# The last block of an expert's tokens: rows of its capacity, or all 128 of its list

## The chip, the core and the metric

The kernel runs on one core of a Trainium2 chip. The metric is the device time of one execution in microseconds (us); the time before is the median of three runs, 435.78 us (433.74 to 437.44). A profiled execution of the same kernel took 432.73 us.

## What is computed

The reference is a retention layer (8 sequences of 576 positions, 8 heads of 64) and behind it a layer of 8 experts in which each token goes to one expert at most. Cut to what matters here:

```python
x = attn_out.transpose(0, 2, 1, 3).reshape(4608, 512)      # the tokens
do_compute = (x @ w_skip) > 0                               # about half of them go on
e_idx = argmax(x[do_compute] @ w_gate, axis=1)              # one expert each
for e in range(8):
    mask = e_idx == e
    h = maximum(xc[mask] @ w1[e], 0)                        # 512 -> 1024
    y[mask] = gate_w[mask, None] * (h @ w2[e])              # 1024 -> 512
out[do_compute] = xc + y
```

All inputs and outputs are 32-bit floats.

## The kernel before, in words

The first part, to about 180 us, computes the retention in groups of 128 tokens (36 groups), writes every token's row of 512 numbers to `out` in HBM, and on the way works out each token's expert and its place in that expert's list. The second part, the expert stage, goes over the experts in order of size, expert 0 being the largest. Each has a fixed capacity, `CAPS = (368, 344, 332, 308, 304, 286, 278, 276)`, and its list is worked on in three blocks of up to 128 rows. `blocks(e)` (L379) gives each block its number of rows `n`: 128, 128 and what is left of the capacity, so the last block has 112, 88, 76, 52, 48, 30, 22 and 20 rows for experts 0 to 7. What is over a capacity is worked on in a loop at the end (L965), which had no round to do in the profiled run.

The list itself (`gidx`, from `slot_ids`, L336) always has 3 x 128 entries for each expert, since every token's place is compared with `iota`, which counts to 384. An entry that no token holds comes out as 0, which is the row of the first token (`max(id - 128, 0)`, L361).

For one expert the steps are:

- gather (L793, through `fetch`, L302): one indirect DMA for each block, on GpSimd's queue, reads the rows of the listed tokens from `out` into `xg[:n, k, :]`, a row on each partition. Expert 0's first two blocks are fetched earlier (L296, with a list of their own), and its last one in `slot_ids` (L351). An expert's gather is issued while the expert before it, or the one before that, is at work.
- turn (L797): TensorE transposes the block so that the 512 features lie on the partitions. The 512 features are four groups of 128 columns (`cs`); for each group and block one transpose takes `xg[:n, k, 128 columns]` as weights and a piece of the unit matrix, `ident[:n, :n]`, as the moving operand. The result lands in a PSUM bank `pt`. Then `split` (L143) writes it as two parts: ScalarE rounds it into `xhi`, VectorE subtracts that from it into `xlo`. One turn call of experts 1 to 7 does one column group, all three blocks; there are four such calls, put between the products of the expert before (L885, `turn_next`). Expert 0's last block is turned alone, in two calls of two column groups each (L938).
- up and down (L390, L809): products of `xhi`, `xlo` with the weights' parts `whi`, `wlo`, three for each pair, in 8 steps `f`. `up` goes into `ph`, is rounded through a relu into `hhi` and `hlo`, and `down` adds into `py`. Both take only the capacity's columns, `xT[:, c, :CAPS[e]]`.
- finish (L833): the result is copied to `yT`, transposed back into `yn` (L840), scaled and added to `xg[:n]` (L842), and scattered to `out` by an indirect DMA, `n` rows (L843).

TensorE's order is written out by hand (`manual_schedule`, L667); the order of the other engines is the scheduler's. Weights come in chunks of 512 KB on SyncE's queue, up to five steps ahead (`AHEAD`), and are split on ScalarE (L139) and VectorE (L140).

In the profile L804 is the transposes of a turn, L144 and L145 its split, L303 every gather, L387 all products of up and down.

Of the kernel before, what the change touches and what calls it, by code (L numbers as in the profile page):

```python
# [23 lines left out]
P = 128  # L24
# [32 lines left out]
def kernel(  # L57
# [9 lines left out]
    nc = tc.nc  # L67
# [25 lines left out]
    ident = const.tile([P, P], F32, tag="ident", name="ident")  # L93
# [49 lines left out]
    def split(hi, lo, x):  # L143
        nc.scalar.copy(hi, x)  # L144
        nc.vector.tensor_tensor(lo, x, hi.bitcast(F32), ALU.subtract)  # L145
# [132 lines left out]
    xg0 = ep.tile([P, NBLK, DM], F32, tag="xg0", name="xg0")  # L278
# [23 lines left out]
    def fetch(dst, idx, nrow=NTOK):  # L302
        nc.gpsimd.indirect_dma_start(  # L303
            out=dst,
            out_offset=None,
            in_=out[:nrow],
            in_offset=bass.IndirectOffsetOnAxis(ap=idx, axis=0),
            bounds_check=nrow - 1,
            oob_is_err=False,
        )  # L310
# [21 lines left out]
    gidx = const.tile([P, NBLK, NE], I32, tag="gidx", name="gidx")  # L332
# [3 lines left out]
    def slot_ids(ps):  # L336

        info = ps[:, 0 : NBLK * NE * NCMP].rearrange("s (b e k) -> s b e k", b=NBLK, k=NCMP)
        pb = [P, NBLK, NE, NE]

        k, n = blocks(0)[-1]
        rl = rt.tile([P, NE, NCMP], F32, tag="rl", name="rl", bufs=1)
        nc.vector.tensor_copy(rl, info[:, k])
        il = rt.tile([P, NE], F32, tag="il", name="il")
        nc.vector.scalar_tensor_tensor(il, rl[:, :, 0], float(P), rl[:, :, 1], ALU.mult, ALU.add)
        nc.vector.tensor_tensor(il, il, lead, ALU.mult)
        ids = rt.tile([P, 1], F32, tag="ids", name="ids")
        nc.vector.tensor_reduce(ids, il, axis=AX.X, op=ALU.add)
        gl = rt.tile([P, 1], I32, tag="gl", name="gl")
        nc.vector.tensor_scalar(gl, ids, float(-P), 0.0, ALU.add, ALU.max)  # L350
        fetch(xg0[:n, k, :], gl[:n])  # L351
        raw = rt.tile([P, NBLK, NE, NCMP], F32, tag="raw", name="raw", bufs=1)
        nc.vector.tensor_copy(raw, info)
        idf = rt.tile([P, NBLK, NE], F32, tag="idf", name="idf")
        nc.vector.scalar_tensor_tensor(idf, raw[:, :, :, 0], float(P), raw[:, :, :, 1], ALU.mult, ALU.add)
        pm = rt.tile(pb, F32, tag="pm", name="pm")
        nc.vector.tensor_tensor(
            pm, idf.unsqueeze(2).broadcast_to(pb), perm.unsqueeze(1).broadcast_to(pb), ALU.mult
        )
        nc.vector.tensor_reduce(idf, pm, axis=AX.X, op=ALU.add)  # L360
        nc.vector.tensor_scalar(gidx, idf, float(-P), 0.0, ALU.add, ALU.max)  # L361
        far = rt.tile([P, NBLK, NE], F32, tag="far", name="far")
        nc.vector.tensor_scalar(far, idf, float(P), FAR, ALU.is_lt, ALU.mult)
        nc.vector.scalar_tensor_tensor(sidx, idf, float(-P), far, ALU.add, ALU.add)
        gs = rt.tile([P, NBLK, NE], F32, tag="gs", name="gs")
        nc.vector.tensor_tensor(gs, raw[:, :, :, 2], raw[:, :, :, 3], ALU.add)
        nc.vector.tensor_tensor(gs, gs, raw[:, :, :, 4], ALU.add)
        pg = rt.tile(pb, F32, tag="pg", name="pg")
        nc.vector.tensor_tensor(
            pg, gs.unsqueeze(2).broadcast_to(pb), perm.unsqueeze(1).broadcast_to(pb), ALU.mult  # L370
        )
        nc.vector.tensor_reduce(gate, pg, axis=AX.X, op=ALU.add)
# [6 lines left out]
    def blocks(e):  # L379
        return [(k, min(P, CAPS[e] - k * P)) for k in range(NBLK)]  # L380
# [368 lines left out]
    def bank(tag, name, bufs=1):  # L749
        return (pm if tag == "m" else mpp).tile([P, 512], F32, tag=tag, name=name, bufs=bufs)  # L750
# [41 lines left out]

    def gather(e, xg, ks):  # L793
        for k, n in ks:
            fetch(xg[:n, k, :], gidx[:n, k, e : e + 1])

    def turn(e, xg, hi, lo, ks, cs, tag):  # L797

        c0, c1 = ks[0][0] * P, ks[-1][0] * P + ks[-1][1]
        w = c1 - c0  # L800
        pt = bank(tag, f"pt_{e}_{cs[0]}_{c0}")[:, : len(cs) * w].rearrange("p (c i) -> p c i", i=w)
        for i, c in enumerate(cs):
            for k, n in ks:
                nc.tensor.transpose(  # L804
                    pt[:, i, k * P - c0 : k * P - c0 + n], xg[:n, k, c * P : (c + 1) * P], ident[:n, :n]
                )
        split(hi[:, cs[0] : cs[-1] + 1, c0:c1], lo[:, cs[0] : cs[-1] + 1, c0:c1], pt)

    def down(e, f, ks, py, h, w):  # L809
        if e == 0:  # L810
# [44 lines left out]
    def gather_next(e, xg):  # L855

        xg[e] = mp.tile([P, NBLK, DM], F32, tag="xg", name=f"xg_{e}", bufs=3)
        gather(e, xg[e], blocks(e))

    def experts(acts):  # L860
# [24 lines left out]
        def turn_next(e):  # L885
            xT[e] = [mp.tile([P, NCC, CAP], F32R, tag=x, name=f"{x}_{e}") for x in ("xhi", "xlo")]
            for c in range(NCC):
                where = ((5, 0), (6, 0), (6, 1), (7, 0))[c] if e == 1 else (3 + c, 0)
                at(e - 1, *where, lambda c=c: turn(e, xg[e], *xT[e], blocks(e), [c], ("pt", "m")[c % 2]))
# [4 lines left out]
        for n in range(len(steps) + 1):  # L894
# [33 lines left out]
            if last and last[2] is late:  # L928
                for f in range(NCUT):
                    down(0, f, late, py[0], hs[0, f], wq[0, f])  # L930
                split_raw(len(raw))
            elif last:
                e, f, ks = last
                if e not in py:
                    py[e] = [bank(f"py{c}", f"py_{e}_{c}") for c in range(NBLK if e == 0 else NCC)]
                if n == NCUT:
                    down(e, f, ks[:1], py[e], hs[e, f], wq[e, f])
                    for cs, tag in (((0, 1), "pt"), ((2, 3), "py3")):  # L938
                        turn(0, xg0, xhi0, xlo0, late, cs, tag)
                    ks = ks[1:]  # L940
                down(e, f, ks, py[e], hs[e, f], wq[e, f])
                if f == NFC - 1:
                    y = evacuate(e, py[e])
                    if e + 1 < NE:
                        for k, where in zip(blocks(e), ((1, 1), (2, 0), (2, 1))):
                            at(e + 1, *where, finish, e, y, xg[e], [k])
                    else:
                        finish(e, y, xg[e], blocks(e), ("pt", "m", "ph"))
# [5 lines left out]
    def rest():  # L954
        routing(0)
        slot_ids(ps_m)
        expert_ids()
        regs[1:] = expert_regs()[1:]
# [6 lines left out]
    with tc.For_i(0, nblock, 1):  # L965
# [28 lines left out]
        for c in range(NCC):  # L994
            turn(0, xg0, xhi0, xlo0, one, [c], ("pt", "py3")[c % 2])
# [69 lines left out]
```

## Time and profile before

| | |
|---|---|
| median of three runs | 435.78 us |
| profiled execution | 432.73 us, of it span 431.0 us |
| PE busy (matmuls) | 391.7 us, 91% of the span |
| transposes of the turns, L804 | 88: 56 of 128x128, 4 each of 112, 88, 76, 52, 48, 30, 22, 20 rows |
| gathers, L303 | 24 indirect DMAs, 948 to 2015 ns of GpSimd each |
| mean granted TensorE clock | 0.983 |

In the rows below, times are us from the span's start unless marked ns. PE is TensorE's matmuls, PEld its weight loads, which overlap the matmuls; DVE is VectorE, ACT ScalarE, POOL GpSimd. A matmul's start is recorded and its end is modelled, and matmuls overlap; so what an operation takes of PE's stream is read from one start to the next, and not from its length. A row "pt<-ident,xg 52*128 52x128" is an operation that writes or feeds `pt` from `ident` and `xg`, with 52 active rows and 128 columns of the array. "idle before <-" names what ended an engine's idle time; "issue" is time in which the profile shows nothing that it waited for.

### The profile page before, as it was taken

The page shows a single profiled execution, that of the slowest core. Times are in us where ns is not written, and L with a number is a line of the kernel's source. Part 1 is how long each engine was busy: PE and PEld are TensorE (multiplying, and loading weights), DVE is VectorE, ACT ScalarE, POOL GpSimd, SP SyncE. Part 2 cuts the span into 40 slices and gives each one's busy share as a digit, 9 for nine tenths or more (in the row PEclk, how much of TensorE's full clock was granted, in tenths as well). Part 3 has the DMA queues.
Part 4 walks back from the last instruction along what each step waited for, and adds up shares of the span by engine and source line. Part 5 has one row for each costly group of instructions (what it writes and reads, how often), then busy time and mean ns, then how long its engine had stood idle before and what let it go on. Part 6 is the DMA issues. An engine that isn't in the chain of part 4 may idle for free. (4 is left out here: it accounts for less than half of the span.)

```text
span 431.0 us, 13306 instructions
## 1 busy us (share of the span) xinstructions
PE 391.7 (91%) x5482; PEld 351.7 (82%) x5484; DVE 276.3 (64%) x562; ACT 186.9 (43%) x360; POOL 160.4 (37%) x182
## 2 busy tenths in 40 slices
PE   7788988899988589999999999999999999999990
PEld 3576776677777467888999999999999999999980
DVE  2595598488589978848755554865654755656430
ACT  2255444454644457117444434444444445445210
POOL 4665564545555397150330042033141250400302
PEclk9899999999999989999999999999999999999996
DMA  8899989899986977255673455455465465642101
GB/s 311 301 326 314 344 304 314 313 327 307 365 310 232 338 284 240 98 149 207 203 230 117 146 172 193 147 173 185 150 212 172 162 207 173 200 144 77 52 0 52
DMA packets 29023, 92.14 MB, mean 214 GB/s; under 512 B 4119, under 2 KB 4247, under 8 KB 28960
## 3 DMA queue, kind: packets, MB, share of 16 engines
q1 hardware_dynamic: 19584, 71.31, 48.4%
q0 software_dynamic: 3616, 9.86, 6.7%
q10 hardware_dynamic: 5760, 10.09, 6.3%
q8 instruction: 44, 0.72, 0.7%
q14 instruction: 19, 0.16, 0.1%
HBM read 77.07 MB, written 14.55 MB: 213 GB/s over the span
## 5 line engine op out<-in xcount | busy, mean ns | idle before, releaser
L140 DVE TENSOR_TENSOR wlo_w<-w,whi_w 128x1024 fp32r<-128x1024 f32 x59 | 71.9, 1223 | 61.9 <-ACT whi_w L139 61.8
L513 POOL TENSOR_TENSOR kn<-u,tt_sb 64x512 f32<-64x512 f32 x72 | 77.3, 1073 | 67.2 <-PE psc L479 44.2
L843 POOL DMA_INDIRECT out<-rs,sidx x24 | 32.8, 1366 | 156.4 <-DVE rs L842 153.2
L139 ACT CAST whi_w<-w 128x1024 fp32r<-128x1024 f32 x59 | 61.6, 1051 | 61.5 <-PE py L387 59.4
L542 ACT COPY u<-ps_s 64x256 f32<-64x256 f32 x128 | 47.0, 367 | 65.6 <-issue 26.7
L387 PE MATMUL py<-hhi,whi_w 128*128 128x344 f32 (+6 forms) x224 | 70.6, 315 | 0.0
L387 PE MATMUL ph<-xhi,whi_w 128*128 128x344 f32 (+6 forms) x224 | 68.9, 308 | 0.0
L387 PE MATMUL py<-hhi,wlo_w 128*128 128x344 f32 (+6 forms) x224 | 67.8, 303 | 0.0
L387 PE MATMUL ph<-xhi,wlo_w 128*128 128x344 f32 (+6 forms) x224 | 67.8, 302 | 0.0
L387 PE MATMUL ph<-xlo,whi_w 128*128 128x344 f32 (+6 forms) x224 | 67.7, 302 | 0.0
L387 PE MATMUL py<-hlo,whi_w 128*128 128x344 f32 (+6 forms) x224 | 67.6, 302 | 0.0
L531 PE MATMUL ps_s<-u,kn 64*64 64x64 f32 x1024 | 48.8, 227 | 14.4 <-issue 6.4
L531 PEld LDWEIGHTS ps_s<-u,kn 64*64 64x64 f32 x1024 | 39.2, 135 | 26.8 <-issue 10.8
L495 DVE TENSOR_TENSOR u<-psc,dt_sb 64x512 f32<-64x512 f32 x72 | 49.6, 689 | 14.2 <-PE psc L479 8.9
L395 ACT ACTIVATE hhi<-ph 128x344 fp32r<-128x344 f32 (+8 forms) x61 | 26.0, 427 | 64.1 <-PE ph L387 57.0
L479 PE MATMUL psc<-u 64*64 64x64 f32 x1152 | 51.8, 227 | 1.9 <-DVE u L495 0.6
L560 PE MATMUL pxt<-u 128*64 128x64 f32 x1152 | 45.1, 231 | 3.2 <-issue 2.8
L479 PEld LDWEIGHTS psc<-u 64*64 64x64 f32 x1152 | 41.7, 136 | 5.3 <-issue 2.4
L560 PEld LDWEIGHTS pxt<-u 128*64 128x64 f32 x1152 | 39.1, 142 | 7.5 <-issue 4.6
L387 PEld LDWEIGHTS py<-hhi,whi_w 128*128 128x128 f32 x224 | 42.2, 188 | 0.9
L387 PEld LDWEIGHTS ph<-xhi,whi_w 128*128 128x128 f32 x224 | 42.3, 189 | 0.1
L387 PEld LDWEIGHTS ph<-xlo,whi_w 128*128 128x128 f32 x224 | 42.3, 189 | 0.1
(178 smaller groups left out, 645.0 us busy)
## 6 DMA issues: line engine op xcount, KB each, us to landing
u<-qkv SPq DMA_DIRECT2D x72, 512.0 KB, 5.2
w<-w SPq DMA_DIRECT2D x64, 512.0 KB, 3.7
out<-xn ACTq DMA_DIRECT2D x36, 256.0 KB, 5.4
out<-rs,sidx POOLq DMA_INDIRECT x24
xg<-out,gidx POOLq DMA_INDIRECT x21
dt_sb<-dtab ACTq DMA_DIRECT2D x1, 256.0 KB
gt_sb<-dtab ACTq DMA_DIRECT2D x1, 256.0 KB
wg_sb<-wg ACTq DMA_DIRECT2D x1, 64.0 KB, 8.8
```

The source lines that it names most:

```text
L139: nc.scalar.copy(hi, t)
L140: nc.vector.tensor_tensor(lo, t, hi.bitcast(F32), ALU.subtract)
L387: nc.tensor.matmul(ps, x, y, start=first and n == 0, stop=last and n == 3 * len(terms) - 1)
L395: nc.scalar.activation(hi, ph, AF.Relu)
L479: nc.tensor.matmul(psc_t[g][halves[j], c, a, :], u[halves[j], 1 - j, c, a, :], u[halves[j], j, c, a, :], start=c == 0 and a == 0, stop=c = ...
L495: nc.vector.tensor_tensor(u_t[g][h, j], psc[halves[j]], dt_sb[h, c0 : c0 + 2], ALU.mult)
L513: nc.gpsimd.tensor_tensor(kn_t[g][h], u_t[g][h, 2 + j], tt_sb[h, 0, c0 : c0 + 2, :].unsqueeze(3).broadcast_to([D, 2, NPR, D]), ALU.mult,)
L531: nc.tensor.matmul(ps_s[halves[j], a, :], kn_t[g][h, c, a, :], u_t[g][h, 3 - j, c, a, :], start=n % NQ == 0 and a == 0, stop=a == NPR - 1, ...
L542: nc.scalar.copy(u_t[g][halves[j], 3 - j, c], ps_s[halves[j]])
L560: nc.tensor.matmul(pxt[halves[j], a, c * D : (c + 1) * D], u_t[g][:, 3 - j, c, a, :], u_t[g][:, j, c, a, :], start=c == 0 and a == 0, stop ...
L843: put = nc.gpsimd.indirect_dma_start(out=out, out_offset=bass.IndirectOffsetOnAxis(ap=sidx[:n, k, e : e + 1], axis=0), in_=rs[:n], in_offs ...
```

## The change

The gather of every block fetches 128 rows, whatever the capacity leaves for the block: the last block's gather takes all 128 entries of its list, in `gather` and, for expert 0, in `slot_ids`. Every transpose of a turn takes 128 rows and the whole unit matrix. The PSUM piece `pt` is as wide as the blocks times 128, and the split reads from it only the columns up to the capacity, as before. Nothing else reads the added rows: up, down and finish keep their sizes.

```diff
--- before.py
+++ after.py
@@ -348,7 +348,7 @@
         nc.vector.tensor_reduce(ids, il, axis=AX.X, op=ALU.add)
         gl = rt.tile([P, 1], I32, tag="gl", name="gl")
         nc.vector.tensor_scalar(gl, ids, float(-P), 0.0, ALU.add, ALU.max)
-        fetch(xg0[:n, k, :], gl[:n])
+        fetch(xg0[:, k, :], gl)
         raw = rt.tile([P, NBLK, NE, NCMP], F32, tag="raw", name="raw", bufs=1)
         nc.vector.tensor_copy(raw, info)
         idf = rt.tile([P, NBLK, NE], F32, tag="idf", name="idf")
@@ -792,19 +792,17 @@
 
     def gather(e, xg, ks):
         for k, n in ks:
-            fetch(xg[:n, k, :], gidx[:n, k, e : e + 1])
+            fetch(xg[:, k, :], gidx[:, k, e : e + 1])
 
     def turn(e, xg, hi, lo, ks, cs, tag):
 
         c0, c1 = ks[0][0] * P, ks[-1][0] * P + ks[-1][1]
-        w = c1 - c0
+        w = len(ks) * P
         pt = bank(tag, f"pt_{e}_{cs[0]}_{c0}")[:, : len(cs) * w].rearrange("p (c i) -> p c i", i=w)
         for i, c in enumerate(cs):
-            for k, n in ks:
-                nc.tensor.transpose(
-                    pt[:, i, k * P - c0 : k * P - c0 + n], xg[:n, k, c * P : (c + 1) * P], ident[:n, :n]
-                )
-        split(hi[:, cs[0] : cs[-1] + 1, c0:c1], lo[:, cs[0] : cs[-1] + 1, c0:c1], pt)
+            for k, _ in ks:
+                nc.tensor.transpose(pt[:, i, k * P - c0 : (k + 1) * P - c0], xg[:, k, c * P : (c + 1) * P], ident)
+        split(hi[:, cs[0] : cs[-1] + 1, c0:c1], lo[:, cs[0] : cs[-1] + 1, c0:c1], pt[:, :, : c1 - c0])
 
     def down(e, f, ks, py, h, w):
         if e == 0:
```

TensorE's order at expert 0's last block (`pt_0_256` and `pt_2_256` are its two PSUM pieces, `xg_130` is expert 0's tile; the shape is that of the output):

```order
 L387 MATMUL py_0_3337<-wlo_w_4_2989_3126,hhi_4_3502 128x512
 L387 MATMUL py_0_3337<-whi_w_4_2989_3125,hlo_4_3503 128x512
-L804 MATMUL pt_0_256_3528<-ident,xg_130 128x112 x2
-L804 MATMUL pt_2_256_3533<-ident,xg_130 128x112 x2
+L804 MATMUL pt_0_256_3528<-ident,xg_130 128x128 x2
+L804 MATMUL pt_2_256_3533<-ident,xg_130 128x128 x2
 L387 MATMUL py_1_3338<-whi_w_4_2989_3125,hhi_4_3502 128x512
 L387 MATMUL py_1_3338<-wlo_w_4_2989_3126,hhi_4_3502 128x512
```

The four transposes stand where they stood, and are of 128 columns in place of 112.

TensorE's order at the first column group of expert 3 (`xg_4094` its tile), which is turned among the products of expert 2:

```order
 L387 MATMUL ph_3_0_4233<-xlo_3894,whi_w_3_3995_3997 128x332
 L387 MATMUL ph_3_0_4233<-xhi_3893,wlo_w_3_3995_3998 128x332
-L804 MATMUL pt_0_0_4250<-ident,xg_4094 128x128 x2
-L804 MATMUL pt_0_0_4250<-ident,xg_4094 128x52
+L804 MATMUL pt_0_0_4250<-ident,xg_4094 128x128 x3
 L387 MATMUL py_0_4144<-hhi_2_4176,whi_w_2_3954_3956 128x332
 L387 MATMUL py_0_4144<-hlo_2_4177,whi_w_2_3954_3956 128x332
```

Three transposes as before, in the same place; the third has 128 columns in place of 52. The same holds for all column groups of experts 1 to 7.

GpSimd's order from expert 0's last gather on, before (`xg_3474`, `xg_3762`, `xg_4094` are the tiles of experts 1, 2 and 3; L843 is the scatter of expert 0's results):

```order
L303 DMA xg_130<-out,gl 112x512
L303 DMA xg_3474<-out,gidx 128x512 x2
L303 DMA xg_3474<-out,gidx 88x512
L303 DMA xg_3762<-out,gidx 128x512 x2
L303 DMA xg_3762<-out,gidx 76x512
L843 DMA out<-rs_0_3820,sidx 4608x512
L843 DMA out<-rs_1_3848,sidx 4608x512
L843 DMA out<-rs_2_3865,sidx 4608x512
L303 DMA xg_4094<-out,gidx 128x512 x2
L303 DMA xg_4094<-out,gidx 52x512
```

And in the changed kernel (L841 is the same scatter):

```order
L303 DMA xg_130<-out,gl 128x512
L303 DMA xg_3474<-out,gidx 128x512 x3
L303 DMA xg_3762<-out,gidx 128x512 x3
L841 DMA out<-rs_0_3820,sidx 4608x512
L841 DMA out<-rs_1_3848,sidx 4608x512
L841 DMA out<-rs_2_3865,sidx 4608x512
L303 DMA xg_4094<-out,gidx 128x512 x3
L841 DMA out<-rs_0_4165,sidx 4608x512
```

The number and the order of the DMAs are the same, and so are the waits of every engine; each last gather has 128 rows. Rows of one shape are now written as one.

## The prediction

> **What bounds the kernel now.** I read the page's head first, then busy time by stretch, then the waits, then the timeline around the turns. The head gives the span and the load of each engine.
>
> ```profile
> span 431.0 us, 13306 instructions
> PE 391.7 (91%) x5482; PEld 351.7 (82%) x5484; DVE 276.3 (64%) x562; ACT 186.9 (43%) x360; POOL 160.4 (37%) x182
> ```
>
> The windows view splits the expert stage, in which experts 1 to 7 are turned. Columns: stretch, its length, busy time and instructions of PE, PEld, DVE, ACT and POOL, granted clock, DMA share, GB/s.
>
> ```profile
> 214.00:243.00 29.00, 29.00 (x191) 28.93 (x190) 15.11 (x21) 13.58 (x21) 4.09 (x4) 1.00 0.54 178
> 304.00:334.00 30.00, 30.00 (x216) 29.12 (x215) 17.20 (x26) 13.99 (x22) 8.31 (x6) 1.00 0.51 175
> 364.00:393.00 29.00, 29.00 (x223) 28.14 (x222) 17.60 (x28) 14.15 (x23) 4.38 (x3) 1.00 0.52 166
> ```
>
> PE is busy for the whole of each stretch at a granted clock of 1.00; VectorE and ScalarE work about half of it and the DMA engines half. But a busy PE need not be a full PE, and the waits from 214 to 393 us say so (waiter, releaser, us in total, times, longest).
>
> ```profile
> ACT whi_w L139 <- PE py L387: 54.2, 42, 1.7
> DVE wlo_w L140 <- ACT whi_w L139: 58.4, 35, 2.0
> PEld pt L804 <- issue: 3.3, 20, 0.2
> ```
>
> The first two rows are engines that wait on PE, or behind one that does; none of the answer's rows has PE waiting for one of them. The third is PE's weight load standing idle 20 times at line 804, the turn, with nothing that the profile shows to wait for. Twenty is four column groups times five experts, and experts 3 to 7 are the five whose last block has fewer than 64 rows (52, 48, 30, 22, 20). The forms at that line are these.
>
> ```profile
> L804 PEld LDWEIGHTS pt<-ident,xg x88: 132/140/144, 185.3 to 385.4; 128*128 128x128 f32 x56, 112*128 112x128 f32 x4, 88*128 88x128 f32 x4, 76*128 76x128 f32 x4
> ```
>
> The timeline shows what a turn takes of PE's stream. Three turns follow: one for expert 2 (last block 76 rows), one for expert 3 (52), one for expert 7 (20). Its merged row "x3" is three blocks, the last the short one. Columns: start, length, engine, line, operation.
>
> ```profile
> 219.53 0.45 PE L804 MATMUL pt<-ident,xg 128*128 128x128 f32 x3
> 219.78 0.40 PE L387 MATMUL py<-hhi,whi_w 128*128 128x344 f32 x1
> 220.02 0.32 PE L387 MATMUL py<-hlo,whi_w 128*128 128x344 f32 x1
> 220.17 0.32 PE L387 MATMUL py<-hhi,wlo_w 128*128 128x344 f32 x1
> ...
> 252.00 0.57 PE L804 MATMUL pt<-ident,xg 128*128 128x128 f32 x3
> 252.50 0.42 PE L387 MATMUL py<-hhi,whi_w 128*128 128x332 f32 x1
> 252.76 0.32 PE L387 MATMUL py<-hlo,whi_w 128*128 128x332 f32 x1
> 252.91 0.32 PE L387 MATMUL py<-hhi,wlo_w 128*128 128x332 f32 x1
> ...
> 385.05 0.54 PE L804 MATMUL pt<-ident,xg 128*128 128x128 f32 x3
> 385.53 0.40 PE L387 MATMUL py<-hhi,whi_w 128*128 128x278 f32 x1
> 385.76 0.29 PE L387 MATMUL py<-hlo,whi_w 128*128 128x278 f32 x1
> 385.89 0.29 PE L387 MATMUL py<-hhi,wlo_w 128*128 128x278 f32 x1
> ```
>
> I charge a turn with the time from its first start to the second product behind it, less one usual spacing of products, because the first product behind a turn starts early and is held. With 76 rows: 220.02 - 219.53 - 0.15 = 0.34 us. With 52 rows: 252.76 - 252.00 - 0.15 = 0.61. With 20 rows: 385.76 - 385.05 - 0.13 = 0.58. Fewer rows cost more: a step between 76 and 52 rows. The weight loads show one half of it, a pause ahead of the short block.
>
> ```profile
> 252.31 0.13 PEld L804 LDWEIGHTS pt<-ident,xg 52*128 52x128 f32 x1 [0.17 <-issue]
> ...
> 374.36 0.13 PEld L804 LDWEIGHTS pt<-ident,xg 20*128 20x128 f32 x1 [0.17 <-issue]
> ```
>
> **The change part by part.** No instruction is added, dropped or moved, and no wait changes. Three things grow: the last block's transposes, its gathers, and the tile in PSUM that the split reads (still only the capacity's columns).
>
> *Transposes of experts 3 to 7.* What a full third block costs is not in the turns of before, but the same kind of transpose stands in the result's turning back, four of 128x128 in a row.
>
> ```profile
> 245.22 0.60 PE L840 MATMUL yn<-ident,yT 128*128 128x128 f32 x4
> 245.57 0.40 PE L387 MATMUL ph<-xhi,whi_w 128*128 128x332 f32 x1
> 245.81 0.32 PE L387 MATMUL ph<-xlo,whi_w 128*128 128x332 f32 x1
> 245.96 0.32 PE L387 MATMUL ph<-xhi,wlo_w 128*128 128x332 f32 x1
> ```
>
> By the same measure four cost 245.81 - 245.22 - 0.15 = 0.44 us, so one 0.11 and three 0.33. A turn of expert 3 so gains 0.61 - 0.33 = 0.28 us and one of expert 7 gains 0.58 - 0.33 = 0.25. With the mean of the ends, 0.265, twenty turns gain 5.3 us. All of it lies on PE, which ends last throughout this stretch, so it comes off the end one for one. What is late next: each step of a product pair is shortened by under 0.3 us four times per expert, while VectorE is busy 17.20 of 30 us and DMA 0.51 of it; neither comes near.
>
> *Transposes of experts 1 and 2.* 88 and 76 rows become 128: 0.34 before against 0.33 for three full ones, so nothing, and I bound the eight turns by one column's price. One full transpose spends 0.11 us on 128 columns, 0.86 ns each; 40 and 52 columns more, four times each, are at most 0.3 us. I take zero, from the row with 76.
>
> *Expert 0's turn and its late gather.* Here PE does wait for data. The gather is issued behind the list at 181.59 us and PE starts on it at 185.31, 3.7 us later.
>
> ```profile
> 181.59 1.29 POOL L303 DMA_INDIRECT xg<-out,gl  x1 [11.32 <-DVE gs L367]
> 185.31 0.57 PE L804 MATMUL pt<-ident,xg 112*128 112x112 f32 x4 [0.62 <-DMA xg<-out,gl]
> ...
> 185.83 1.06 POOL L303 DMA_INDIRECT xg<-out,gidx  x1 [0.31 <-issue]
> 193.14 0.46 PE L804 MATMUL pt<-ident,xg 128*128 128x128 f32 x3
> ...
> 354.70 0.95 POOL L303 DMA_INDIRECT xg<-out,gidx  x1 [0.30 <-issue]
> ...
> DMA packets 29023, 92.14 MB, mean 214 GB/s; under 512 B 4119, under 2 KB 4247, under 8 KB 28960
> ```
>
> Sixteen more rows of 2 KB are 32 KB; at the mean of 214 GB/s that is 0.15 us, and nothing if they ride beside the others. Four transposes grow by 16 columns of 0.86 ns, 0.05 us together. I take 0.1 us for both, range 0 to 0.2.
>
> *The other gathers.* POOL spends 1.06 us on the 88 rows issued at 185.83 and 0.95 us on the 20 rows at 354.70, so its time hardly hangs on the rows, and POOL is busy at most 28% of a stretch (8.31 of 30 us). What a gather lands later is covered: expert 1's last block, at 3.7 us from issue, is there at 189.5 and first used at 193.1; expert 7's at 358.4 and used at 374.36. Nothing on the path, as long as 3.6 us of cover hold. All capacities together gain 576 rows (16+40+52+76+80+98+106+108), 1.2 MB against 92.14.
>
> *Sum.* -5.3 + 0.1 = -5.2 us, with ends at -4.8 (full 0.3 at experts 1 and 2, and 0.2 at expert 0) and -5.3. The profiled execution took 432.73 us, its span and 1.73 us around it, so 427.5 by its own measure. It ran 0.7% below the median of the three timed runs, 435.78; on that scale the forecast is 430.6 us.
>
> A rule that speaks against the change stands in the Trainium skill, page "TensorE: Matmul & The Clock Gate", section "Why this matters for your kernels": a single matmul with a contraction of 32 takes as long as one with 128. By it the short blocks would hold nothing to win. The rows disagree: 0.61 us with 52 rows, 0.34 with 76.
>
> **The rivals.**
>
> *A, half the pause stays.* The 3.3 us ahead of the short block go, but the rest stays, because it belongs to the passage from transposes to products and not to the row count. Then 435.78 - 3.3 + 0.1 = 432.6 us. Against it: the passage behind four full transposes is in the 0.44 us already, and that is 0.11 each with nothing left over.
>
> *B, the gain is taken back.* With PE faster, the weights' way (load, round on ScalarE, subtract on VectorE) sets the pace: 435.8 us. Against it: ScalarE waits 54.2 us for PE in this stretch.
>
> *C, the length decides.* If a transpose costs by its columns and the pauses come of something that stays, 576 rows times four groups at 0.86 ns add 2.0 us: 437.8 us. For it: the four full transposes of line 840 do run at one even spacing of 0.11 us, so columns have a price. Against it: the five experts that pause are just the five under 64 rows. The Trainium skill's rule above points this way.
>
> *D, slower: the longer gathers land late.* The added list entries are mostly empty slots, which the kernel points to row 0, so many reads go to one row. If they were served one after another at r ns each, expert 1 (40 rows, cover 3.6 us) and expert 7 (108 rows, cover 374.36 - 358.4 = 16.0 us) would be the first to stop PE, from 90 and 148 ns on. At 200 ns that is 4.4 + 5.6 = 10.0 us, less the 5.2: 440.6 us, and experts 5 and 6 could only add. It turns the change to a loss from about 167 ns a row on. One of the 16 DMA engines, at a sixteenth of 214 GB/s, takes 153 ns for 2 KB, so only a nearly serial service would do it; what speaks for it is only that no gather of before has an added entry to show.
>
> That the change does not do what it says I leave out: the blocks of 128 rows stand in the order of the instructions.
>
> **How the numbers follow.** The forecast has a chance of 0.77, A 0.08, B 0.05, C 0.04, D 0.06. The predicted time is the forecast's 430.6 us. The three runs of before lie within 0.5% of their median, so about 1% is what a measurement can tell from no change; 1% below 435.78 is 431.4, only 0.8 us above the forecast. A median of three may well be off by that, so of the forecast's chance I give a fifth to "within 1%". Faster: 0.62. Same: 0.15 + A, B and C = 0.32. Slower: D, 0.06. Range: the forecast with the runs' spread (433.74 to 437.44, so about -2.0 and +1.7, and 0.4 of the sum's upper end) reaches from 428.5 to 432.7 and takes in A; I go up to 433.3 for a part of B, and leave B, C and D outside.
>
> **What would show it.** Right: line 804 has 84 transposes of 128x128 of experts 1 to 7 and 4 of expert 0, all one form; no row of PEld waiting at the turn in the expert stage; a turn of expert 3 costs 0.33 us by the measure above; the stretch from expert 3's first turn (252.00) to expert 7's last (385.05) is shorter by about 5 us; PE still busy all through. Wrong: a pause that stays behind the turn (A), waits of PE on the weights (B), turns of 0.6 us and more (C), PE waiting for a gather ahead of expert 1 or 7 (D), or more than 0.2 us added to the 0.62 us wait at expert 0.

## The result and the profile after

The changed kernel takes 429.63 us (median of four runs, 426.02 to 429.80) against 435.67 us for the kernel before: a ratio of 0.987, 95% interval 0.982 to 0.992. In a second series it took 429.46 us (twelve runs) against 433.78 us (23 runs): 0.991, interval 0.987 to 0.995. The ratios leave out runs more than 1.5% above the fastest of their kernel, while the medians are of all runs, so a ratio can differ from the quotient of two medians. The forecast was 430.6 us.

First the page's head, the form at the turn's line, PE's one wait that is left there (for expert 0's gather; PEld has one too, 0.8 us at the same place), and the DMA line of the changed kernel.

```profile
span 428.0 us, 13306 instructions
PE 387.8 (91%) x5482; PEld 351.6 (82%) x5484; DVE 274.6 (64%) x562; ACT 186.0 (43%) x360; POOL 156.6 (37%) x182
...
L804 PEld LDWEIGHTS pt<-ident,xg x88: 137/141/145, 187.8 to 382.6; 128*128 128x128 f32 x88
...
PE pt L804 <- DMA xg<-out,gl: 0.4, 1, 0.4
...
DMA packets 29135, 93.32 MB, mean 218 GB/s; under 512 B 3961, under 2 KB 4089, under 8 KB 29072
```

All 88 transposes have one form. The line on which the argument stood, PEld idle 20 times for 3.3 us, is gone: from 214 to 393 us no row of the waits has PE or PEld as the waiter. The first and the last start of that row give the length of the turns' stretch: 382.6 - 187.8 = 194.8 us, where before it was 385.4 - 185.3 = 200.1 us. That is 5.3 us less, the forecast's main term. The gathers move 1.18 MB more.

The turns of expert 3 and expert 7 in the changed kernel, from the timeline:

```profile
254.56 0.49 PE L804 MATMUL pt<-ident,xg 128*128 128x128 f32 x3
254.81 0.40 PE L387 MATMUL py<-hhi,whi_w 128*128 128x332 f32 x1
255.04 0.32 PE L387 MATMUL py<-hlo,whi_w 128*128 128x332 f32 x1
255.19 0.32 PE L387 MATMUL py<-hhi,wlo_w 128*128 128x332 f32 x1
...
372.29 0.49 PE L804 MATMUL pt<-ident,xg 128*128 128x128 f32 x3
372.54 0.37 PE L387 MATMUL py<-hhi,whi_w 128*128 128x278 f32 x1
372.75 0.29 PE L387 MATMUL py<-hlo,whi_w 128*128 128x278 f32 x1
372.88 0.29 PE L387 MATMUL py<-hhi,wlo_w 128*128 128x278 f32 x1
```

By the prediction's measure (first start to the second product behind, less one spacing) they cost 255.04 - 254.56 - 0.15 = 0.33 us and 372.75 - 372.29 - 0.13 = 0.33 us, where they were 0.61 and 0.58.

The stretch starts 2.5 us later than in the profile of before (187.8 against 185.3), so the span fell by 3.0 us and not by 5.3. That part lies ahead of anything that the change touches; the last experiments show how far it scatters by itself.

### The profile page after: what moved, and what is told of

It is laid out like the page before. It is cut to its first block, busy times and chain, and to the rows that moved or that the text cites. A ratio compares the mean times of both kernels' runs of the same rounds, so it can differ in the third digit from the quotient of the medians.

```text
span 428.0 us, 13306 instructions
## 1 busy us (share of the span) xinstructions
PE 387.8 (91%) x5482; PEld 351.6 (82%) x5484; DVE 274.6 (64%) x562; ACT 186.0 (43%) x360; POOL 156.6 (37%) x182
## 4 chain that ended last, share of the span: by engine, by line
PE 29%; DMA 21%; issue 12%; DVE 4%; POOL 3%; POOLq 0%; DVEq 0%
DMA out<-rs,sidx 15%; PE py L387 11%; PE ph L387 10%; DMA xg<-out,gidx 3%; POOL out L841 2%; PE ps_s L531 1%; PE pxt L560 1%; DMA xg<-out,gi 1%; PE pt L804 1%; POOL xg L303 1%; PE ph_early L387 1%; DVE u L495 1%; PE ph L404 1%; PE px L584 1%; DMA xg<-out,gl 1%
## 5 line engine op out<-in xcount | busy, mean ns | idle before, releaser
L841 POOL DMA_INDIRECT out<-rs,sidx x24 | 32.7, 1362 | 153.2 <-DVE rs L840 150.0
L531 PE MATMUL ps_s<-u,kn 64*64 64x64 f32 x1024 | 49.7, 230 | 12.6 <-issue 7.3
L479 PE MATMUL psc<-u 64*64 64x64 f32 x1152 | 53.0, 230 | 3.4 <-issue 2.2
L479 PEld LDWEIGHTS psc<-u 64*64 64x64 f32 x1152 | 42.7, 139 | 4.9 <-issue 2.3
L573 DVE TENSOR_TENSOR xt<-pxt,gt_sb 128x512 f32<-128x512 f32 x36 | 24.8, 688 | 27.7 <-PE pxt L560 27.4
```

Source lines behind the costliest of these rows:

```text
L479: nc.tensor.matmul(psc_t[g][halves[j], c, a, :], u[halves[j], 1 - j, c, a, :], u[halves[j], j, c, a, :], start=c == 0 and a == 0, stop=c = ...
L531: nc.tensor.matmul(ps_s[halves[j], a, :], kn_t[g][h, c, a, :], u_t[g][h, 3 - j, c, a, :], start=n % NQ == 0 and a == 0, stop=a == NPR - 1, ...
L573: nc.vector.tensor_tensor(xt_t[b][:, :, o * P : (o + 1) * P].rearrange("p a (c i) -> p a c i", c=2), pxt.rearrange("p a (c i) -> p a c i", ...
L841: put = nc.gpsimd.indirect_dma_start(out=out, out_offset=bass.IndirectOffsetOnAxis(ap=sidx[:n, k, e : e + 1], axis=0), in_=rs[:n], in_offs ...
```

## Experiments

The theory: a transpose of 64 rows or fewer, between others of 128, makes PE pause at the change to it and at the change back, about 0.27 us for the pair. The rivals: the fuller gathers bring the gain; the pause falls evenly with the rows; it comes of the short moving operand; it belongs to each short transpose, or to the end of a turn, and not to the change. Each run has a profile, and the stretch of the turns (200.1 us before, 194.8 us after) tells a turn's cost far more finely than the whole time does. In all twelve profiles the granted clock from 180 to 393 us is 1.00, so their stretches can be compared.

**The gathers alone.**

```diff
-        fetch(xg0[:n, k, :], gl[:n])
+        fetch(xg0[:, k, :], gl)
...
-            fetch(xg[:n, k, :], gidx[:n, k, e : e + 1])
+            fetch(xg[:, k, :], gidx[:, k, e : e + 1])
```

> Only the gathers take 128 rows; the turns keep their short blocks. Theory (a pause of about 0.27 us around each of the 20 transposes with 64 rows or fewer): the pauses stay, so a turn of expert 3 still takes 0.61 us, PEld still waits 20 times at the turn, and the stretch from the first to the last start at the turn's line stays at 200.1 us; device time as before, within 0.3%. Rival (the gain came from the fuller gathers, for example because the DMA engines split them evenly): the stretch falls to about 194.8 us and the time by 1.3%. The cost of the added rows alone should be under 0.2 us.

The turn's row and its waits:

```profile
L804 PEld LDWEIGHTS pt<-ident,xg x88: 133/140/144, 189.2 to 389.3; 128*128 128x128 f32 x56, 112*128 112x128 f32 x4, 88*128 88x128 f32 x4, 76*128 76x128 f32 x4
...
  issue: 4.4, 21
  DMA xg<-out,gl: 0.7, 1
```

Stretch 200.1 us, the pauses in place (4.4 us, of which about 1.1 is the one at expert 0). The gathers bring nothing, and no row of the stretch is longer for the added 576 rows. But the whole time was 437.4 us against 436.2 us of before, and the ratio is 1.009 with an interval of 1.004 to 1.014, beyond the 0.3% expected, which the stretch does not explain. I come back to it below.

**64 rows, and 65.** Gather and turn of the last block take `max(n, 64)` rows, then `max(n, 65)`; the split still reads the capacity's columns. The edit for 64, and the same with 65:

```diff
-            fetch(xg[:n, k, :], gidx[:n, k, e : e + 1])
+            m = max(n, 64)
+            fetch(xg[:m, k, :], gidx[:m, k, e : e + 1])
...
             for k, n in ks:
+                m = max(n, 64)
                 nc.tensor.transpose(
-                    pt[:, i, k * P - c0 : k * P - c0 + n], xg[:n, k, c * P : (c + 1) * P], ident[:n, :n]
+                    pt[:, i, k * P - c0 : k * P - c0 + m], xg[:m, k, c * P : (c + 1) * P], ident[:m, :m]
                 )
```

> Gather and turn of the last block take max(n, 64) rows: experts 3 to 7 have 64 in place of 52, 48, 30, 22, 20. Theory with the step at 64 rows: the pauses stay; a turn of experts 3 to 7 takes 0.61 us or a little more, and the stretch of the turns is 200.1 to 200.6 us. Rival (the pause shrinks evenly as a block grows to 128): about half of it goes, 0.45 us a turn and 197.5 us.

> The same with max(n, 65) rows: one row more than the run before it. Theory with the step at 64 rows: all pauses go, a turn takes 0.33 us, no wait of PEld at the turn, stretch 194.8 us, time 1.2% under before. Rival (even growth): as with 64 rows, about 197.5 us; rival (the step lies at 65 to 76 rows): 200.1 us as before.

The turn's row with 64 rows, then expert 3's turn of it (weight load of the short block, then the products):

```profile
L806 PEld LDWEIGHTS pt<-ident,xg x88: 134/140/144, 190.9 to 391.4; 128*128 128x128 f32 x56, 64*128 64x128 f32 x20, 112*128 112x128 f32 x4, 88*128 88x128 f32 x4
...
257.56 0.58 PE L806 MATMUL pt<-ident,xg 128*128 128x128 f32 x3
...
258.33 0.32 PE L387 MATMUL py<-hlo,whi_w 128*128 128x332 f32 x1
258.49 0.32 PE L387 MATMUL py<-hhi,wlo_w 128*128 128x332 f32 x1
...
257.87 0.13 PEld L806 LDWEIGHTS pt<-ident,xg 64*128 64x128 f32 x1 [0.17 <-issue]
```

And with 65:

```profile
L806 PEld LDWEIGHTS pt<-ident,xg x88: 137/140/146, 189.8 to 384.6; 128*128 128x128 f32 x56, 65*128 65x128 f32 x20, 112*128 112x128 f32 x4, 88*128 88x128 f32 x4
...
256.48 0.44 PE L806 MATMUL pt<-ident,xg 128*128 128x128 f32 x3
...
256.96 0.32 PE L387 MATMUL py<-hlo,whi_w 128*128 128x332 f32 x1
257.12 0.31 PE L387 MATMUL py<-hhi,wlo_w 128*128 128x332 f32 x1
```

With 64 rows a turn costs 258.33 - 257.56 - 0.16 = 0.61 us and the stretch is 200.5 us, 0.4 longer than before, since the short blocks are longer. With 65 it costs 256.96 - 256.48 - 0.16 = 0.32 us and the stretch is 194.8 us, that of the full change. One row more takes the whole pause away; nothing falls evenly. The whole times point the same way: a ratio of 1.011 (1.002 to 1.020) with 64 rows, 0.986 (0.979 to 0.993) with 65. The 1.1% over before is more than the stretch's 0.4 us can explain; it came in the same series as the 0.9% of the gathers alone. The last 63 rows of the change buy nothing that the profile shows.

**Rows or columns.** In a transpose both shrink together, so here the last block of experts 3 to 7 goes through a plain product instead, once with 128 rows and n columns of the unit matrix, once with n rows and 128 columns. Both fetch all 128 rows.

Against the changed kernel, short in columns:

```diff
-            for k, _ in ks:
-                nc.tensor.transpose(pt[:, i, k * P - c0 : (k + 1) * P - c0], xg[:, k, c * P : (c + 1) * P], ident)
+            for k, n in ks:
+                x = xg[:, k, c * P : (c + 1) * P]
+                if n > 64:
+                    nc.tensor.transpose(pt[:, i, k * P - c0 : (k + 1) * P - c0], x, ident)
+                else:
+                    nc.tensor.matmul(pt[:, i, k * P - c0 : k * P - c0 + n], x, ident[:, :n], start=True, stop=True)
```

The same, short in rows:

```diff
+            for k, n in ks:
+                x = xg[:, k, c * P : (c + 1) * P]
+                o = pt[:, i, k * P - c0 : (k + 1) * P - c0]
...
+                else:
+                    nc.tensor.matmul(o, x[:n], ident[:n], start=True, stop=True)
```

> As the changed kernel, but the last block of experts 3 to 7 is turned by a plain product of all 128 rows with only n columns of the unit matrix (52 to 20): full in rows, short in the moving operand. Theory (rows decide): no wait of PEld at the turn, the short block as dear as a plain product is, without a pause in front of it. Rival (the short moving operand decides): 20 waits of about 0.17 us stay.

> The mirror of it: the last block of experts 3 to 7 is turned by a plain product of only n rows (52 to 20) with all 128 columns of the unit matrix's first n rows. Theory (rows decide): 20 waits of PEld of about 0.17 us stand at the turn, and the turn is about 0.27 us dearer than in the run with short columns. Rival (the moving operand decides): no waits.

Expert 3's turn, short in columns:

```profile
260.72 0.38 PE L806 MATMUL pt<-ident,xg 128*128 128x128 f32 x2
260.93 0.32 PE L808 MATMUL pt<-ident,xg 128*128 128x52 f32 x2
261.08 0.40 PE L387 MATMUL py<-hhi,whi_w 128*128 128x332 f32 x1
261.31 0.31 PE L387 MATMUL py<-hlo,whi_w 128*128 128x332 f32 x1
261.47 0.31 PE L387 MATMUL py<-hhi,wlo_w 128*128 128x332 f32 x1
```

Short in rows:

```profile
252.10 0.38 PE L807 MATMUL pt<-ident,xg 128*128 128x128 f32 x2
252.41 0.48 PE L809 MATMUL pt<-ident,xg 52*128 52x128 f32 x2
252.82 0.43 PE L387 MATMUL py<-hhi,whi_w 128*128 128x332 f32 x1
253.09 0.32 PE L387 MATMUL py<-hlo,whi_w 128*128 128x332 f32 x1
253.24 0.32 PE L387 MATMUL py<-hhi,wlo_w 128*128 128x332 f32 x1
...
252.41 0.29 PEld L809 LDWEIGHTS pt<-ident,xg 52*128 52x128 f32 x2 [0.17 <-issue]
...
  issue: 3.3, 20
```

A plain product of these floats shows as two passes, so its own cost is higher. Short in columns there is no wait at the turn in the expert stage, and the turn costs 261.31 - 260.72 - 0.16 = 0.43 us. Short in rows the 20 waits of 3.3 us are back, and it costs 253.09 - 252.10 - 0.15 = 0.84 us. So the rows decide. That short columns of the weights do no harm either, the result's transposes show: the changed kernel has them with 128 rows and down to 20 columns, and the waits from 214 to 420 us list for them one idle time of PE and PEld, 0.3 us behind VectorE. The difference, 0.41 us, is more than the 0.27 expected; the moving operand differs too (128 columns against 52, twice), and these two runs don't separate its part. Both ran once (438.29 and 437.30 us), so their whole times say nothing.

**The change or the short transpose.** First each short block is transposed twice, once between the two full ones:

```diff
-            for k, n in ks:
+            for k, n in [ks[0], ks[2], ks[1], ks[2]] if ks[-1][1] <= 64 else ks:
```

> As before, but in experts 3 to 7 the short block is transposed twice in each turn, once between the first and the second full block and once behind them (the second writes the same values again). Theory (each change between full and short costs): two more changes in each of 20 turns, so each turn grows by another 0.27 us and the short transpose's own 0.11, about 1.0 us in place of 0.61, PEld waits 40 times, stretch 200.1 + 7.6 = 207.7 us. Rival (the pause belongs to the end of a turn, whatever the rows): only the added transpose counts, 0.11 us each, stretch 202.3 us.

Expert 3's turn, its weight loads from the first short block on, and the turn's row:

```profile
250.73 0.92 PE L804 MATMUL pt<-ident,xg 128*128 128x128 f32 x4
251.58 0.42 PE L387 MATMUL py<-hhi,whi_w 128*128 128x332 f32 x1
251.84 0.32 PE L387 MATMUL py<-hlo,whi_w 128*128 128x332 f32 x1
251.99 0.32 PE L387 MATMUL py<-hhi,wlo_w 128*128 128x332 f32 x1
...
250.93 0.59 PEld L804 LDWEIGHTS pt<-ident,xg 52*128 52x128 f32 x3 [0.21 <-issue]
...
L804 PEld LDWEIGHTS pt<-ident,xg x108: 133/138/148, 184.0 to 390.6; 128*128 128x128 f32 x56, 52*128 52x128 f32 x8, 48*128 48x128 f32 x8, 30*128 30x128 f32 x8
```

The turn costs 251.84 - 250.73 - 0.15 = 0.96 us, the stretch 206.6 us. The added transpose with its two changes is worth 0.35 us in expert 3 and (206.6 - 200.1) / 20 = 0.33 on the mean; less the 0.11 of a full transpose that leaves 0.22 for a pair of changes among transposes, under the 0.27 expected, and far from none. Before's pair, reckoned in the same way, is a little dearer; that this is because it comes back into products is not shown. The profile counts 20 waits of PEld, not the 40 expected. Its row from 250.93 shows why: it merges the short, the second full and the second short load over 0.59 us, of which three loads of 0.13 to 0.14 us fill some 0.41. The other 0.18 us are idle time too, in pieces that the waits do not list. The whole time rose to 441.43 us, a ratio of 1.023 (1.014 to 1.033), which is more than the stretch's 6.5 us.

Then the other way: before's sizes, but the short blocks of experts 3 to 7 go through a fifth call that turns their four column groups one behind the other.

```diff
-                at(e - 1, *where, lambda c=c: turn(e, xg[e], *xT[e], blocks(e), [c], ("pt", "m")[c % 2]))
+                ks = blocks(e) if e < 3 else blocks(e)[:2]
+                at(e - 1, *where, lambda c=c, ks=ks: turn(e, xg[e], *xT[e], ks, [c], ("pt", "m")[c % 2]))
+            if e > 2:
+                at(e - 1, 6, 1, lambda: turn(e, xg[e], *xT[e], blocks(e)[2:], list(range(NCC)), "pt"))
```

> Before's sizes, but the short blocks of experts 3 to 7 are not turned in each of the four calls; a fifth call turns all four column groups of the last block one behind the other. Theory (a pause belongs to a change between full and short, not to each short transpose): 5 pairs of changes in place of 20, so about 15 x 0.27 = 4.0 us less than before on PE, less the cost of a fifth passage from transposes to products for each expert (under 0.1 us each), stretch about 196.5 us, time about 0.8% under before. Rival (each short transpose has its own pause): 200.1 us as before.

The waits of the stage, a turn of the two full blocks, the four short blocks of expert 3 with their weight loads, and the range of the starts at the turn's and at the result's transposes:

```profile
PEld pt L804 <- issue: 0.9, 5, 0.2
...
256.05 0.38 PE L804 MATMUL pt<-ident,xg 128*128 128x128 f32 x2
...
256.42 0.32 PE L387 MATMUL py<-hlo,whi_w 128*128 128x332 f32 x1
256.58 0.32 PE L387 MATMUL py<-hhi,wlo_w 128*128 128x332 f32 x1
...
262.09 0.45 PE L804 MATMUL pt<-ident,xg 52*128 52x52 f32 x4
262.46 0.42 PE L387 MATMUL ph<-xhi,whi_w 128*128 128x332 f32 x1
262.72 0.31 PE L387 MATMUL ph<-xlo,whi_w 128*128 128x332 f32 x1
...
262.08 0.32 PEld L804 LDWEIGHTS pt<-ident,xg 52*128 52x128 f32 x4 [0.20 <-issue]
...
L804 PEld LDWEIGHTS pt<-ident,xg x88: 132/140/144, 181.6 to 378.5; 128*128 128x128 f32 x56, 112*128 112x128 f32 x4, 88*128 88x128 f32 x4, 76*128 76x128 f32 x4
L840 PEld LDWEIGHTS yn<-ident,yT x84: 91/139/145, 241.3 to 410.6; 128*128 128x128 f32 x56, 128*88 128x88 f32 x4, 128*76 128x76 f32 x4, 128*52 128x52 f32 x4
```

Five waits in place of 20: four short transposes in a row share one pair of changes. The turn's cost says the same without the count: the two full blocks cost 256.42 - 256.05 - 0.16 = 0.21 us, the four short ones together 262.72 - 262.09 - 0.15 = 0.48, so a column group costs 0.21 + 0.48 / 4 = 0.33 us, as in the changed kernel, where it was 0.61 before. The four short weight loads, each 0.13 to 0.14 us long, span 0.32 us, so they start some 0.06 us apart, where full transposes are 0.11 apart: a short block by itself is the cheaper one, and what costs is the change. The stretch is 378.5 - 181.6 = 196.9 us as expected (196.5). Since the last turn stands elsewhere here, the fairer length is from the first turn to the last transpose of a result: 410.6 - 181.6 = 229.0 us. The result's transposes of the changed kernel, then of before:

```profile
L838 PEld LDWEIGHTS yn<-ident,yT x84: 91/138/145, 247.6 to 416.3; 128*128 128x128 f32 x56, 128*88 128x88 f32 x4, 128*76 128x76 f32 x4, 128*52 128x52 f32 x4
```

```profile
L840 PEld LDWEIGHTS yn<-ident,yT x84: 91/139/145, 245.1 to 419.0; 128*128 128x128 f32 x56, 128*88 128x88 f32 x4, 128*76 128x76 f32 x4, 128*52 128x52 f32 x4
```

The changed kernel needs 416.3 - 187.8 = 228.5 us for that length, the kernel before 419.0 - 185.3 = 233.7 us. So 4.7 of the 5.2 us come without one more row gathered. The whole times are less sure: a ratio of 0.991 (0.986 to 0.996), but medians of 432.11 against 433.93 us, only 0.4% apart. It does not beat the change.

**Whole times and the part ahead.** The kernel before and the changed one once more, and the gathers alone with more rounds.

> The kernel before, unchanged, once more with a profile. If the scatter of whole times comes from the part ahead of the expert stage, the turn of expert 0 begins a few us off 185.3 us, while the stretch of the turns is 200.05 us again within 0.1 us.

> The changed kernel, unchanged, with more rounds. Stretch of the turns 194.9 us within 0.1; time 1.2% under before; the start of expert 0's turn free to lie some us off.

> Only the gathers take 128 rows, once more with more rounds, since its first timing was 0.9% over before with no row of the expert stage longer. If that was scatter of the part ahead (theory): ratio within 0.5% of 1, stretch 200.0 us. If the added rows do cost (rival): the ratio is 1.005 to 1.013 again, and some wait of the profile is longer by some 3 us than in before.

The turn's row of the kernel before, again:

```profile
L804 PEld LDWEIGHTS pt<-ident,xg x88: 132/140/144, 184.2 to 384.3; 128*128 128x128 f32 x56, 112*128 112x128 f32 x4, 88*128 88x128 f32 x4, 76*128 76x128 f32 x4
```

The changed kernel, again:

```profile
L804 PEld LDWEIGHTS pt<-ident,xg x88: 137/140/145, 187.3 to 382.2; 128*128 128x128 f32 x88
```

The early transposes of expert 0's first blocks, which lie ahead of every edit here, in the first run of the gathers alone and in the run with one fifth call:

```profile
L620 PEld LDWEIGHTS pt_early<-ident,xg x8: 138/140/143, 169.2 to 171.1; 128*128 128x128 f32 x8
```

```profile
L620 PEld LDWEIGHTS pt_early<-ident,xg x8: 139/140/143, 162.0 to 163.5; 128*128 128x128 f32 x8
```

The stretch repeats within 0.1 us: 200.1 us for the kernel before, 194.9 for the changed one, 200.0 for the gathers alone. What scatters is the retention part: the early transposes begin at 169.2 us in one run and 162.0 in another with the same instructions ahead of them. That is more than the whole effect of the change. Those two are different kernels, but one and the same kernel scatters too: the gathers alone have these transposes at 169.2 us in the first profile and at 166.0 in the second, and the runs of the kernel before in this series took 429.20 to 439.08 us. Its own profiles lie closer, 165.6 and 164.7, so that the turn of expert 0 began 1.1 us earlier and not a few us. With more rounds the gathers alone came to 434.74 against 433.78 us, ratio 0.997 (0.993 to 1.002): the 0.9% of the first timing did not repeat, and I take it for scatter. The changed kernel came out at 0.991, 0.9% under before where 1.2% was expected. What in the retention part scatters stays open. The granted clock alone is not it: up to 162 us its mean was 0.97 both in the run with 169.2 and in the one with 162.0.

## Why the prediction was right

- *Transposes of experts 3 to 7*, 5.3 us from 20 turns: 5.3 us (200.1 to 194.8). The price of a full third block, taken from the result's transposes, held to the hundredth: 0.33 us.
- *Transposes of experts 1 and 2*, taken as nothing with up to 0.3 us: nothing. Expert 2's turn costs as much as expert 3's, 0.33 us.
- *Expert 0's turn and late gather*, 0.1 us: PE's wait for it was 0.4 us after against 0.6 before, and its four transposes cost 0.47 us against 0.43.
- *The other gathers*, nothing: the gathers alone left the stretch at 200.1 us.
- *The sum* of -5.2 us against the median of before gave 430.6; 429.63 and, in the second series, 429.46 us were measured. The medians moved by 6.0 and by 4.3 us: the sum lies between. That 430.6 came within 1.2 us of both times is in part luck, since the runs of one kernel lie up to 10 us apart (429.20 to 439.08); the 5.3 us of the stretch are not. On the profiled execution's own scale, 427.5 was forecast and 429.72 measured, because its part ahead was 2.5 us longer; the sum's own ends (0.4 us up, 0.1 down) were a small part of the doubt, the runs' spread the large one.
- *Rival A* (half stays) fell: no wait of PEld is left at the turn in the stage, and the turn is at 0.33 us. *Rival B* (the weights take over) fell: no row of the waits has PE waiting from 214 to 393 us. *Rival C* (the length decides) fell in the rows of 64 and 65, where a longer block is the cheaper. *Rival D* (gathers land late) fell: PE waits for no gather but expert 0's.
- The rule of the Trainium skill that spoke against the change, page "TensorE: Matmul & The Clock Gate", section "Why this matters for your kernels" (a contraction of 32 takes as long as one of 128), does not price a short one among full ones: 0.61 us with 64 rows, 0.32 with 65. What the runs show agrees with the Trainium skill's page "TensorEngine Tiling (Array Packing)", section "Key Properties" under "Tiling Modes", by which a change of the tiling mode drains the engine, and with its list of modes, in which 64 rows is the step under 128. That the pause is such a drain is only argued, from the step at 64 and from the pauses that follow the changes; no row names the mode.
- The chance of 0.62 for more than 1%: the first series lies beyond the bound, the second just inside it. An effect of 1.2% under a scatter of this size had to be a near thing.

## What to carry to other kernels

Where short blocks of 64 rows or fewer stand between full ones in PE's stream, read the starts across them: a short block can cost more than a full one, and here 65 rows were enough to be rid of it. Where padding is dear, group the short ones, so that they share one pair of changes. A change that touches one stage is best measured in that stage, by two starts of the trace, when another stage scatters by more than the effect.

## What the hardware showed that I had not expected

The step is as sharp as it can be: 64 rows 0.61 us a turn, 65 rows 0.32. Over the price of a full transpose, a pair of changes among transposes costs 0.22 us, less than the 0.27 about the last block of a turn. Four short transposes in a row follow one another at 0.06 us, half the spacing of full ones. And the retention part, with the same instructions, ended between 162.0 and 172.8 us over the twelve profiles, by the start of the transposes behind it. The row below is the latest, the run with short columns; its mean granted clock up to 162 us was 0.92, the lowest of the twelve.

```profile
L620 PEld LDWEIGHTS pt_early<-ident,xg x8: 138/140/143, 172.8 to 175.4; 128*128 128x128 f32 x8
```
